# Attention and two expert layers on one core: another order at the start, tanh for sigmoid, column tiles, other buffers at two stage borders, a last product in halves

## The chip, the core and the metric

The kernel runs on one NeuronCore of one Trainium2 chip. A core has TensorE (matmuls; its weight loads are a row of their own in a profile, PEld), VectorE (DVE), ScalarE (ACT), GpSimd (POOL) and SyncE (SP), whose instruction queue issues most of the DMA transfers here. The metric is the time of one execution on the device in microseconds (us); the median of several runs counts.

## What is computed

All inputs and the output are float32 in the reference except that the weights arrive as float64 words. The kernel computes a linear attention and two expert layers behind it, for 8 x 576 = 4608 tokens:

```python
q_s = softmax(q, axis=-1)              # q, k, v: (8, 8, 576, 64): batch, head, token, 64
k_s = softmax(k, axis=2)               # over the tokens
kv  = einsum('bhsd,bhse->bhde', k_s, v)
x   = einsum('bhsd,bhde->bhse', q_s, kv)   # then (4608, 512)
h   = x @ w1_in                        # (4608, 2048)
g   = h * (1 / (1 + exp(-1.702 * h)))
x1  = g @ w1_out                       # (4608, 512)
h2  = x1 @ w2_in                       # (4608, 2048)
g2  = where(h2 >= 1, h2, where(h2 <= -1, 0, (h2 + 1)**2 / 4))
out = g2 @ w2_out                      # (4608, 512)
```

## The kernel before

All large products run on float32 split in a high and a low half (`split`, L103: ScalarE copies the high half, L104, VectorE subtracts to get the low half, L105), as three matmuls: high by high, high by low, low by high. A weight arrives as 64-bit words; `conv` (L85) makes float32 of it with one ScalarE copy (L92) and three VectorE operations (L94, L95, L99).

**First stage** (`x @ w1_in`, plain). Tokens come in 9 blocks j of 512, the 2048 columns of h in 16 groups m of 128; step s is (j, m), with twelve matmuls (`gemm1`, L767 to L769). After every second step `act` (L771) applies the sigmoid on ScalarE (L775), multiplies on VectorE (L776) and stores g. The attention of the next block is prepared beside the steps of the present one, by `chain` (L785), which puts each operation on a step: `load_k`, `k_max`, `k_col` (a transpose, then a maximum, L664), `k_sub` (L672), `k_exp` (L681); `load_v`; `k_v` (L683: per head pair, five matmuls of 128 rows of keys by 129 columns, two heads at once and a column of ones for the sum; the last of the five has 64 rows); `load_q`, `q1` (maximum and subtraction, L707 and L708), `q1e` (exponential, L711), `q2` (sum L716, reciprocal, multiply), `q3` (transposes and a copy), `q4` (matmuls px and a split). The exponentials are put on two steps per block, so that those between two sigmoids run together. For block 0 all of this stands ahead of the first step (L837 to L872). The weights of w1_in are loaded and converted in 16 groups (`load_w`, `conv_w`), the first ahead of the steps, the others in the steps of block 0. In later blocks the weights of the other three products are converted and combined by `weight_sets`.

**The other three products** (out1, in2, out2) use seven block products instead of eight (Winograd's form), named PROD = (1, 7, 6, 2, 5, 4, 3), on tokens in five pieces j (512, 512, 512, 384, 384 tokens per half). A pool of 27 numbered tiles (`slot`) holds all operands; which tile holds what is written out by hand (G_AT, R_AT, O_AT, C_AT, E_AT, L245 to L251). `out_pass(ph, ...)` (L297) is out1 (ph 0) and out2 (ph 1); a step is one product p and one inner quarter i, twelve matmuls at L338. `ready(s)` splits the operands of a step into two tiles, three steps ahead. For ph 1, steps 0 to 3 go to tiles 8 to 15, all later ones round R_AT[1]. `store` sends results out; in out2 it first transposes them (`turn`, L354), copies them into tile 23 (L365) and stores from there. `pass_in` (L434) is in2 with its matmuls at L456; it ends each result with `finish` (ScalarE L470, L471, VectorE L472), in the tiles 22 to 26 (E_AT) round, from which g1 is stored. Beside it the weights of out2 are loaded raw (`load_set`), converted and combined; these jobs stand at steps 14 + 14 i and on. The raw loads use one tile of the pool.

The order of instructions on each engine follows program order as far as a scheduler of the framework leaves it; `behind` ties one instruction behind another.

## Time and profile before

| | |
|---|---|
| median of 3 runs | 1609.55 us (1609.12 to 1614.41) |
| the profiled execution | 1607.64 us, its span 1605.8 us |
| TensorE busy | 1565.2 us (97%) |
| VectorE busy | 1150.5 us (72%) |
| ScalarE busy | 947.4 us (59%) |
| mean granted TensorE clock | 0.996 |
| HBM traffic | 205 GB/s over the span |

The span is the time from the first to the last instruction; some 2 us lie around it. Matmuls overlap, so TensorE's busy share says only where it had work in hand, and the distance from one matmul's start to the next says what one costs. A product step of 12 matmuls of 512 columns takes 2.72 us, of 384 columns 2.08 us.

### The profile page before, as it was taken

How to read it: one execution, taken by the hardware profiler on the slowest of the kernel's cores; microseconds unless marked ns; L12 is line 12 of the kernel's file. 1: busy time of each engine (PE TensorE's matmuls, PEld its weight loads, DVE VectorE, ACT ScalarE, POOL GpSimd, SP SyncE). 2: the span in 40 equal slices, each digit the busy share in tenths (PEclk: the TensorE clock that was granted, in tenths of full speed). 3: DMA queues.
4: the chain of work that ended last, by engine and by line, in shares of the span. 5: the costliest groups of instructions: out<-in, count | busy, mean ns of one | idle time of the engine just before them, and what ended most of it. 6: DMA issues, size and time to landing. Idle time of an engine off the chain costs nothing.

```text
span 1605.8 us, 20662 instructions
## 1 busy us (share of the span) xinstructions
PE 1565.2 (97%) x7588; PEld 1343.1 (84%) x7588; DVE 1150.5 (72%) x1519; ACT 947.4 (59%) x1135; POOL 8.1 (1%) x45
## 2 busy tenths in 40 slices
PE   5899999999999999999999999999999999999998
PEld 3678888888888888888999888878998788888998
DVE  7999788788833678686777686868454876766673
ACT  4877777776832444443545687868775444444453
POOL 0000000000000000000000000000000000000000
PEclk9999999999999999999999999999999999999999
DMA  8788788888767761715368766566547853424421
GB/s 209 217 249 273 257 269 267 275 264 266 254 240 280 270 210 65 225 45 177 101 206 327 274 217 248 203 220 236 193 165 296 328 185 105 157 84 138 131 68 40
DMA packets 218869, 330.61 MB, mean 206 GB/s; under 512 B 90128, under 2 KB 162832, under 8 KB 216080
## 3 DMA queue, kind: packets, MB, share of 16 engines
q1 hardware_dynamic: 218768, 329.30, 60.9%
q8 instruction: 59, 0.97, 0.2%
q14 instruction: 42, 0.34, 0.1%
HBM read 190.84 MB, written 138.41 MB: 205 GB/s over the span
## 4 chain that ended last, share of the span: by engine, by line
PE 89%; DMA 3%; DVE 2%; ACT 1%; issue 1%; SPq 0%; DVEq 0%; ACTq 0%
PE z L338 24%; PE zx L338 18%; PE z L456 10%; PE hps L767 8%; PE hps L769 8%; PE hps L768 8%; PE zx L456 7%; PE pk L689 2%; PE px L738 2%; DMA s<-in_moe_w_out_dram 1%; PE pt L361 1%; DMA g<-s 1%; PE pt L728 1%; DMA wp_out<-s 1%; DVE s L118 0%
## 5 line engine op out<-in xcount | busy, mean ns | idle before, releaser
L104 ACT ACTIVATE s<-s 128x1024 fp32r<-128x1024 f32 (+2 forms) x363 | 326.0, 901 | 370.9 <-PE z L338 177.7
L105 DVE TENSOR_TENSOR s<-s,s 128x1024 fp32r<-128x1024 f32 (+2 forms) x363 | 369.5, 1023 | 175.3 <-PE z L338 71.5
L338 PE MATMUL z<-s,w 128*128 128x512 f32 (+1 forms) x1920 | 404.0, 369 | 5.4 <-DVE s L105 3.3
L338 PEld LDWEIGHTS z<-s,w 128*128 128x128 f32 x1920 | 350.1, 188 | 51.2 <-DVE s L105 3.6
L338 PE MATMUL zx<-s,w 128*128 128x512 f32 (+1 forms) x1440 | 303.2, 368 | 0.0
L338 PEld LDWEIGHTS zx<-s,w 128*128 128x128 f32 x1440 | 261.7, 188 | 33.3
L767 PE MATMUL hps<-xh,w 128*128 128x512 f32 x576 | 237.6, 413 | 5.2 <-ACT w L104 4.6
L769 PE MATMUL hps<-xh,w 128*128 128x512 f32 x576 | 226.5, 393 | 1.1 <-DVE w L105 1.1
L768 PE MATMUL hps<-xl,w 128*128 128x512 f32 x576 | 225.9, 392 | 0.0
L118 DVE TENSOR_TENSOR s<-s,s 128x1024 f32<-128x1024 f32 (+2 forms) x196 | 205.8, 1058 | 21.5 <-DMA s<-g 17.1
L456 PE MATMUL z<-s,w 128*128 128x512 f32 (+1 forms) x960 | 206.9, 367 | 0.0
L456 PEld LDWEIGHTS z<-s,w 128*128 128x128 f32 x960 | 175.1, 188 | 22.6
L456 PE MATMUL zx<-s,w 128*128 128x512 f32 (+1 forms) x720 | 158.9, 369 | 2.8 <-DVE s L118 1.7
L456 PEld LDWEIGHTS zx<-s,w 128*128 128x128 f32 x720 | 130.5, 188 | 22.6 <-DVE s L118 3.9
L767 PEld LDWEIGHTS hps<-xh,w 128*128 128x128 f32 x576 | 108.8, 189 | 31.5 <-ACT w L104 5.6
L776 DVE TENSOR_TENSOR sg<-hps,sg 128x1024 f32<-128x1024 f32 x72 | 87.6, 1217 | 66.3 <-ACT sg L775 66.0
L769 PEld LDWEIGHTS hps<-xh,w 128*128 128x128 f32 x576 | 108.3, 188 | 25.9 <-DVE w L105 2.2
L768 PEld LDWEIGHTS hps<-xl,w 128*128 128x128 f32 x576 | 108.6, 189 | 21.2 <-issue 1.1
L775 ACT ACTIVATE sg<-hps 128x1024 f32<-128x1024 f32 x72 | 73.9, 1026 | 82.4 <-PE hps L769 82.0
L471 ACT ACTIVATE s<-s 128x1024 f32<-128x1024 f32 (+1 forms) x80 | 77.6, 971 | 1.5
L470 ACT ACTIVATE s<-s,half 128x1024 f32<-128x1024 f32 (+1 forms) x40 | 42.4, 1061 | 26.0 <-DVE s L118 25.8
L472 DVE SCALAR_TENSOR_TENSOR s<-s,s 128x1024 f32<-128x1024 f32 (+1 forms) x40 | 44.7, 1116 | 12.4 <-ACT s L471 12.0
(76 smaller groups left out, 1242.4 us busy)
## 6 DMA issues: line engine op xcount, KB each, us to landing
s<-g SPq DMA_DIRECT2D x96, 512.0 KB, 4.4
g<-sg SPq DMA_DIRECT2D x72, 512.0 KB, 3.2
w<-wp_out SPq DMA_DIRECT2D x14, 2048.0 KB, 12.8
g<-s SPq DMA_DIRECT2D x48, 512.0 KB, 2.8
s<-g SPq DMA_DIRECT2D x48, 384.0 KB, 3.8
wp_out<-w SPq DMA_DIRECT2D x28, 512.0 KB, 4.2
wp_in<-w SPq DMA_DIRECT2D x28, 512.0 KB, 3.9
w<-wp_in SPq DMA_DIRECT2D x7, 2048.0 KB, 8.3
```

Source lines behind the costliest of these rows:

```text
L104: nc.scalar.activation(out=hi, in_=src, func=ACTF.Copy)
L105: return nc.vector.tensor_tensor(out=lo, in0=src, in1=hi.bitcast(FP32), op=ALU.subtract)
L118: return nc.vector.tensor_tensor(out=o, in0=x, in1=y, op=op)
L338: nc.tensor.matmul(out=z[:, m, :n], lhsT=a, rhs=b[:, c, :], start=(p in OPENS and i == 0 and c == 0 and x == 0), stop=(i == 3 and c == 1 a ...
L456: nc.tensor.matmul(out=z[:, m, :n], lhsT=a, rhs=b[:, c, :], start=(p in OPENS and c == 0 and x == 0), stop=(c == 1 and x == 2), skip_group ...
L471: nc.scalar.activation(out=t, in_=t, func=ACTF.Square)
L472: nc.vector.scalar_tensor_tensor(out=t, in0=h, scalar=1.0, in1=t, op0=ALU.max, op1=ALU.min)
L767: nc.tensor.matmul(out=hps, lhsT=wh, rhs=xh[:, kk, :], start=(kk == 0), stop=False)
L768: nc.tensor.matmul(out=hps, lhsT=wh, rhs=xl[:, kk, :], start=False, stop=False)
L769: nc.tensor.matmul(out=hps, lhsT=wl, rhs=xh[:, kk, :], start=False, stop=(kk == KD - 1))
L775: nc.scalar.activation(out=sg, in_=hps, func=ACTF.Sigmoid, scale=1.702)
L776: nc.vector.tensor_tensor(out=sg, in0=hps, in1=sg, op=ALU.mult)
```

## The change

- *Start*: the loads of q and v for tiles 0 and 1 are issued from ScalarE's queue, all k loads come ahead of the first w1_in load on SP, the first weight conversion is tied behind the last subtraction of k of block 0, and the q tiles 1 and 2 take their exponentials per head on ScalarE with a bias and a sum (`q1s`).
- *Exponentials*: in `chain` each exponential stands one step behind its subtraction, on its own.
- *tanh for sigmoid*: the first layer stores h (tanh(0.851 h) + 1), twice the wanted value; out1's copies and additions multiply by 0.5.
- *Column tiles*: in `k_v` each head has its own matmul of 64 weight columns by 65 columns, the second head on the array's upper columns; v gets a column of ones per head.
- *in2*: jobs of the raw loads start at step 12 + 14 i, and each load stands two steps ahead of its conversion instead of one; the sums come a step earlier.
- *Entry of out2*: steps 0 to 5 have tiles of their own (4 and 5: 20, 21 and 24, 23) and the round behind them has another order.
- *End of out2*: the last product is computed for its first 128 rows (m = 0) over all four quarters, then for the others; each half is copied, transposed and stored by itself, the last one with ScalarE and VectorE side by side.

```diff
     def conv(raw, f, r):
-        nc.vector.tensor_scalar(out=r, in0=lw, ...)
+        first = nc.vector.tensor_scalar(out=r, in0=lw, ...)
...
+        return first
...
-    R_AT = ((16, 17, 18, 19, 24, 25, 26), (24, 25, 26, 8, 9, 10, 11))
+    R_AT = ((16, 17, 18, 19, 24, 25, 26), (8, 9, 10, 11, 25, 26, 24))
...
+        first_at = ((8, 9), (10, 11), (12, 13), (14, 15), (20, 21), (24, 23))
...
-            if ph and s < 4:
-                at = (8 + 2 * s, 9 + 2 * s)
+            if ph and s < len(first_at):
+                at = first_at[s]
+            elif ph and s >= len(steps) - 4:
+                at = (i, 16 + i)
             else:
-                k = 2 * (s - 4 * ph)
+                k = 2 * (s - len(first_at) * ph)
...
-        def gemm(s):
+        def gemm(s, ms=range(2)):
...
-            for m in range(2):
+            for m in ms:
...
         def turn():
-            for j, a, b, t in late:
+            for j, a, b, t, ms in late:
...
                 for r in range(4):
-                    for m in range(2):
+                    for m in ms:
...
-                nc.scalar.activation(out=u[:n4], in_=pt[:n4], func=ACTF.Copy)
+                d = slice(ms[0] * P, (ms[-1] + 1) * P)
+                if ms == (1,):
+                    nc.scalar.activation(out=u[:n4, :2, d], in_=pt[:n4, :2, d], func=ACTF.Copy)
+                    nc.vector.tensor_copy(out=u[:n4, 2:, d], in_=pt[:n4, 2:, d])
+                else:
+                    nc.scalar.activation(out=u[:n4, :, d], in_=pt[:n4, :, d], func=ACTF.Copy)
...
+        def close(m):
+            n = HALVES[-1]
+            z = zs["x"][:, m, :n]
+            t = tmp["c12"] = tmp["c12"] if m else slot(20)[:, :, :n]
+            c = n // 2 if m else n
+            nc.scalar.activation(out=t[:, m, :c], in_=z[:, :c], func=ACTF.Copy)
+            if m:
+                nc.vector.tensor_copy(out=t[:, m, c:], in_=z[:, c:])
+            late.append((NJ - 1, 0, 1, t, (m,)))
...
-                nc.scalar.activation(out=t, in_=z, func=ACTF.Copy)
+                nc.scalar.activation(out=t, in_=z, func=ACTF.Copy, scale=1.0 if ph else 0.5)
...
+            def more(t):
+                if ph:
+                    tt(t, t, z, ALU.add)
+                else:
+                    nc.vector.scalar_tensor_tensor(
+                        out=t, in0=z, scalar=0.5, in1=t, op0=ALU.mult, op1=ALU.add
+                    )
...
+                for m in range(2):
+                    for i in range(4):
+                        gemm(whole + i, (m,))
+                        if m == 0 and i == 0:
+                            ready(whole + 3)
+                        if i == 2:
+                            turn()
+                    close(m)
                 turn()
...
-            s0 = 14 + i * 14
+            s0 = 12 + i * 14
             for h in range(2):
-                jobs.setdefault(s0 + 2 * h, []).append((load_set, ("out2", i, h)))
-                jobs.setdefault(s0 + 2 * h + 1, []).append((convert_set, (h,)))
+                jobs.setdefault(s0 + 3 * h, []).append((load_set, ("out2", i, h)))
+                jobs.setdefault(s0 + 3 * h + 2, []).append((convert_set, (h,)))
             for part in range(4):
-                jobs.setdefault(s0 + 5 + part, []).append((sum_set, ("out2", i, part)))
+                jobs.setdefault(s0 + 6 + part, []).append((sum_set, ("out2", i, part)))
...
-        v_t = [vpool.tile([P, KR + 1, P + 1], FP32, name=f"v{i}") for i in range(HP)]
+        v_t = [vpool.tile([P, KR + 1, 2, D + 1], FP32, name=f"v{i}") for i in range(HP)]
...
-            conv(raw1(m), f, r)
+            behind(conv(raw1(m), f, r), st["sub"] if m == 0 else None)
...
-            follow(nc.scalar.activation(out=kt, in_=kt, func=ACTF.Exp), st.get(("sub", b)))
+            nc.scalar.activation(out=kt, in_=kt, func=ACTF.Exp)
...
-            pk = ps_a.tile([P, P + 1], FP32, tag="a", name="pk")
+            pk = ps_a.tile([P, D + 1], FP32, tag="a", name="pk")
             for r in range(KR + 1):
                 n = P if r < KR else KT
-                nc.tensor.matmul(
-                    out=pk,
-                    lhsT=kt[:n, r].rearrange("p h d -> p (h d)"),
-                    rhs=vt[:n, r, :],
-                    start=(r == 0),
-                    stop=(r == KR),
-                )
+                for h in range(2):
+                    nc.tensor.matmul(
+                        out=pk[h * D:(h + 1) * D],
+                        lhsT=kt[:n, r, h, :],
+                        rhs=vt[:n, r, h, :],
+                        start=(r == 0),
+                        stop=(r == KR),
+                        tile_position=(0, h * D),
+                        skip_group_check=True,
+                    )
...
+        def q1s(t):
+            qt = q_t[t]
+            mx = sm.tile([P, H], FP32, tag="qm", name="qm")
+            nc.vector.tensor_reduce(out=mx, in_=qt, axis=AX.X, op=ALU.max)
+            nc.vector.tensor_scalar(out=mx, in0=mx, scalar1=-1.0, scalar2=None, op0=ALU.mult)
+            z = st["qz", t] = sm.tile([P, H, 1], FP32, tag="qz", name="qz")
+            for h in range(H):
+                nc.scalar.activation(
+                    out=qt[:, h, :], in_=qt[:, h, :], func=ACTF.Exp, bias=mx[:, h:h + 1], accum_out=z[:, h]
+                )
...
-            nc.scalar.activation(out=sg, in_=hps, func=ACTF.Sigmoid, scale=1.702)
-            nc.vector.tensor_tensor(out=sg, in0=hps, in1=sg, op=ALU.mult)
+            nc.scalar.activation(out=sg, in_=hps, func=ACTF.Tanh, scale=0.851)
+            nc.vector.scalar_tensor_tensor(
+                out=sg, in0=sg, scalar=1.0, in1=hps, op0=ALU.add, op1=ALU.mult
+            )
...
-                    put(4.2 if i < 2 else 8.2, k_exp, b, i)
+                    put(2 * i + 3, k_exp, b, i)
...
-                put(4.3 if i < 2 else 8.3, q1e, t)
+                put(2 * i + 3.3, q1e, t)
...
-        load_k(0, 0)
-        load_k(0, 1)
+        for i in range(HP):
+            load_k(0, i)
+            if i < 2:
+                load_q(i, nc.scalar)
+                load_v(0, i, nc.scalar)
         load_w(0)
-        load_k(0, 2)
-        load_k(0, 3)
...
-        for i in range(HP):
+        for i in range(2, HP):
             load_q(i)
             load_v(0, i)
...
-            q1(i)
-            q1e(i)
+            if i in (1, 2):
+                q1s(i)
+            else:
+                q1(i)
+                q1e(i)
```

## Rows read from the trace of the kernel before

**Rows 1.** Stages: us; PE, PEld, DVE, ACT, POOL busy; clock; DMA share; GB/s.

```profile
0.00:38.18 38.18, 18.20 (x73) 12.80 (x73) 26.58 (x69) 16.70 (x31) 3.25 (x21) 0.96 0.82 206
38.18:103.31 65.13, 58.64 (x274) 45.35 (x273) 63.26 (x126) 50.80 (x72) 0.80 (x4) 1.00 0.78 233
103.31:533.90 430.59, 430.59 (x2046) 351.08 (x2045) 316.00 (x556) 280.27 (x359) 4.01 (x20) 1.00 0.79 265
533.90:878.70 344.80, 344.80 (x1680) 305.51 (x1680) 259.69 (x240) 161.49 (x170) 0.00 (x0) 1.00 0.51 174
878.70:1229.90 351.20, 348.42 (x1686) 305.68 (x1686) 235.34 (x302) 261.25 (x322) 0.00 (x0) 1.00 0.62 221
1229.90:1245.90 16.00, 10.67 (x46) 8.25 (x45) 7.14 (x8) 5.34 (x7) 0.00 (x0) 0.89 1.03 422
...
1598.70:1605.80 7.10, 1.08 (x8) 0.83 (x8) 0.00 (x0) 1.83 (x2) 0.00 (x0) 0.90 0.36 106
```

**Rows 2.** VectorE's waits, 0 to 38.15 us: waiter, releaser, us in total, times, longest.

```profile
DVE m L654 <- DMA kr<-in_k_dram: 4.1, 2, 3.7
DVE w L94 <- DMA w<-in_moe_w_in_dram: 2.8, 1, 2.8
DVE rs L697 <- PE pk L689: 2.6, 2, 1.4
DVE kt L672 <- PE pk L689: 1.1, 1, 1.1
```

**Rows 3.** Groups by line, whole span, then start: busy us, mean ns | idle.

```profile
L775 ACT ACT_TABLE_LOAD x39 | 50.0, 1283 | 0.7
...
L708 DVE TENSOR_TENSOR qt<-qt,qm 128x512 f32<-128x512 f32 x4 | 2.7, 670 | 0.0
```

**Rows 4.** Timeline of TensorE around a pk product: start, duration (us), engine, line, tiles.

```profile
191.72 1.47 PE L689 MATMUL pk<-v,kt 128*128 128x129 f32 x10
...
192.28 0.49 PE L689 MATMUL pk<-v,kt 128*128 128x129 f32 x3
...
192.70 0.49 PE L689 MATMUL pk<-v,kt 64*128 64x129 f32 x2
...
193.45 0.40 PE L769 MATMUL hps<-xh,w 128*128 128x512 f32 x1
```

**Rows 5.** Timeline of a 64-column matmul pair; groups of weight loads by shape.

```profile
91.11 0.33 PE L738 MATMUL px<-qT,kv 128*128 128x64 f32 x2
...
L361 PEld LDWEIGHTS pt<-ident,s 128*128 128x128 f32 x96 | 11.2, 140 | 1.5
...
L361 PEld LDWEIGHTS pt<-ident,s 128*96 128x96 f32 x64 | 7.2, 126 | 1.6 <-ACT s L385 1.2
```

**Rows 6.** VectorE's waits in the in2 stage; the chain there (start, us, what).

```profile
DVE s L94 <- DMA s<-in_moe_w_out_dram: 22.2, 11, 4.6
...
908.84 2.72 PE zx L456 x12
...
920.75 4.75 DMA s<-in_moe_w_out_dram
```

**Rows 7.** Entry of out2: chain, timeline (idle before, releaser), stretches with clock.

```profile
1230.68 13.87 DMA g<-s
...
1242.13 0.50 PE L338 MATMUL z<-s,w 128*128 128x512 f32 x1 [2.06 <-ACT s L104]
...
1245.93 12.53 PE L338 MATMUL z<-s,w 128*128 128x512 f32 x47 [3.30 <-DVE s L105]
...
1245.90:1249.30 3.40, 3.37 (x8) 2.70 (x9) 3.40 (x4) 1.75 (x2) 0.00 (x0) 0.50 0.95 407
1249.30:1252.70 3.40, 3.40 (x16) 2.81 (x16) 3.40 (x4) 2.13 (x2) 0.00 (x0) 0.99 0.98 405
```

**Rows 8.** Timeline of the end.

```profile
1598.73 0.81 ACT L385 ACTIVATE s<-zx 128x768 f32<-128x768 f32 x1 [1.04 <-PE zx L338]
...
1600.83 1.02 ACT L365 ACTIVATE s<-pt 96x1024 f32<-96x1024 f32 x1 [1.29 <-DMA out_dram<-s]
```

More of the change, by code (lines that the diff above doesn't have):

```diff
@@ L92, in conv @@
         nc.scalar.activation(out=f, in_=hwf, func=ACTF.Copy, scale=2.0 ** -112)
-        nc.vector.tensor_scalar(out=r, in0=lw, scalar1=2.0 ** -29, scalar2=7.0, op0=ALU.mult, op1=ALU.min)
+        first = nc.vector.tensor_scalar(
+            out=r, in0=lw, scalar1=2.0 ** -29, scalar2=7.0, op0=ALU.mult, op1=ALU.min
+        )
         nc.vector.scalar_tensor_tensor(
@@ L329, in gemm @@
             z = zs[Z_OF[p]]
-            hi, lo = ops.pop(s)
+            hi, lo = ops[s]
             w = sl[p]
-            for m in range(2):
+            for m in ms:
                 for c in range(2):
@@ L351, in store @@
             else:
-                late.append((j, a, b, t))
+                late.append((j, a, b, t, (0, 1)))
         def turn():
-            for j, a, b, t in late:
+            for j, a, b, t, ms in late:
                 n, t0 = HALVES[j], STARTS[j]
@@ L397, in post @@
             elif p == 5:
-                tt(tmp["s7"], tmp["s7"], z, ALU.add)
+                more(tmp["s7"])
                 store(j, 1, 1, tmp["s7"])
             elif p == 4:
-                tt(tmp["u2"], tmp["u2"], z, ALU.add)
+                more(tmp["u2"])
                 store(j, 1, 0, tmp["u2"])
@@ L410, in run @@
                 ready(s)
-            for s, (j, p, i) in enumerate(steps):
+            whole = len(steps) - 4 * ph
+            for s, (j, p, i) in enumerate(steps[:whole]):
                 gemm(s)
@@ L599, with load_tokens @@
         k_t, q_t, st = {}, {}, {}
-        def load_tokens(dst, src, together):
+        def load_tokens(dst, src, together, eng):
             if together:
-                nc.sync.dma_start(out=dst[:, :, :KR], in_=src[:, :KR * P].rearrange("h (p r) d -> p h r d", r=KR))
+                eng.dma_start(out=dst[:, :, :KR], in_=src[:, :KR * P].rearrange("h (p r) d -> p h r d", r=KR))
             else:
                 for i in range(2):
-                    nc.sync.dma_start(out=dst[:, i, :KR], in_=src[i, :KR * P].rearrange("(p r) d -> p r d", r=KR))
-            nc.sync.dma_start(out=dst[:KT, :, KR], in_=src[:, KR * P:].rearrange("h p d -> p h d"))
+                    eng.dma_start(out=dst[:, i, :KR], in_=src[i, :KR * P].rearrange("(p r) d -> p r d", r=KR))
+            eng.dma_start(out=dst[:KT, :, KR], in_=src[:, KR * P:].rearrange("h p d -> p h d"))
         def load_k(b, hp):
@@ L630, in segs, with load_q @@
                 done += n
-        def load_q(t):
+        def load_q(t, eng=nc.sync):
             qt = qpool.tile([P, H, D], FP32, tag="q", name="qt")
             for off, n, b, s in segs(t * P, P, S):
-                nc.sync.dma_start(
+                eng.dma_start(
                     out=qt[off:off + n], in_=q[b, :, s:s + n, :].rearrange("h p d -> p h d")
@@ L638, in load_q @@
             q_t[t] = qt
-        def follow(ins, other):
-            if other is not None:
-                tc.add_manual_dep(
-                    getattr(ins, "ins", ins),
-                    getattr(other, "ins", other).name,
-                    mybir.DependencyInfo(mybir.DependencyClass.NoSync, mybir.DependencyReason.DATA),
-                    reason="exponentials together",
-                )
         def k_max(b, hp):
@@ L701, in k_v @@
                 o = slice(j * D, (j + 1) * D)
-                nc.scalar.activation(out=kv[o, hp, o], in_=pk[o, o], func=ACTF.Copy, scale=rs[o])
+                nc.scalar.activation(out=kv[o, hp, o], in_=pk[o, :D], func=ACTF.Copy, scale=rs[o])
         def q1(t):
@@ L714, in q2 @@
             qt = q_t[t]
-            z = sm.tile([P, H, 1], FP32, tag="qz", name="qz")
-            nc.vector.tensor_reduce(out=z, in_=qt, axis=AX.X, op=ALU.add)
+            z = st.pop(("qz", t), None)
+            if z is None:
+                z = sm.tile([P, H, 1], FP32, tag="qz", name="qz")
+                nc.vector.tensor_reduce(out=z, in_=qt, axis=AX.X, op=ALU.add)
             nc.vector.tensor_scalar(out=z, in0=z, scalar1=EPS, scalar2=None, op0=ALU.add)
```

18 lines of the change are left out of this document (9 added, 9 removed).

## The prediction

> **What bounds the kernel now.** The stage table comes first [rows 1]: it splits the span by stage and shows which engine has no slack in each. TensorE is busy for all of 103.3 to 533.9 us and all of the out1 product (533.9 to 878.7), at a full clock, so there only its own instructions count and faster neighbours buy nothing. It is not full in four places, and the change works on all four. Until 38.18 us the first token block is prepared and no product runs; VectorE works 26.58 of these 38.18 us. From 38.18 to 103.31 us, the sixteen column groups of the first block, TensorE is busy 58.64 of 65.13 us while VectorE is busy 63.26: here VectorE is the bound. The in2 stage takes 351.2 us where out1, the same 1680 matmuls, takes 344.8. After it TensorE idles over 5 us at the entry of the last product, and 7.1 us follow its last matmul. The waits name the causes, and come next.
>
> **How times are counted.** The sum is made against the profiled execution: 1607.6 us, of which 1605.8 are the span. The median of the runs is 1609.55, 1.9 above it; what the sum takes off is taken off the median.
>
> **Start and first block.** In program order VectorE would do the four k tiles first; in the trace it stood 2.8 us at L94, the first weight group's conversion, until its load landed, with k work queued behind it; 2.6 us at L697 and 1.1 us at L672 it waited for the pk products [rows 2]. The new tie of that conversion behind the last k subtraction takes the 2.8 us away. The pk product needs v, and the v and q loads of tiles 0 and 1 now start at once on ScalarE's queue instead of after nine other issues on SP's; I count all of the 1.1 us and half of the 2.6 us. What is moved: eight DMA issues onto ScalarE ahead of its first exponential (it is idle there, so I cost them at nothing; were it busy they would cost its work their issue time), and on SP the first w1_in load now stands behind all k loads, which hurts nobody since its conversion is moved too. Tiles 1 and 2 take their exponentials on ScalarE with bias and sum: VectorE loses two subtractions (670 ns) and two sums of the same size [rows 3] and gains two tiny operations, 2.4 us net; ScalarE gets 16 short instructions for 2 long ones, beside idle time. ScalarE also drops table loads of 1.28 us each [rows 3] in the first block, where TensorE's idle time is mostly for weights that ScalarE copies. But what it copies comes from VectorE, which has under 2 us of slack in this stage [rows 1]; table loads alone give little, and I count nothing. A DMA rule of the Trainium skill (DMA: Bandwidth & Descriptors, "Rules for kernel authors") speaks against the second load queue: issuing from several engines saves issue time only, since the same 16 DMA engines carry all. The trace bears it out in that these engines are already 0.82 busy in this stretch [rows 1]; by it the queue would give only order, which is all that I count. Sum: 2.8 + 1.1 + 1.3 + 2.4 = 7.6 us. Because VectorE also bounds the block that follows, this moves the whole rest of the program. Bounds: 1 (VectorE meets other waits instead) to 10.3 us (38.18 - 26.58 = 11.6 of idle time, less the 3.7 until k first lands [rows 2], and the 2.4).
>
> **Column tiles.** One pk product is ten matmul records (float32 goes in two passes). From the first at 191.72 to the second GEMM matmul behind it, less that one's own 0.23, it costs 193.45 - 0.23 - 191.72 = 1.50 us [rows 4]. Records lie 0.11 apart (three take 0.49 with the last one's 0.27 in it), ten are 1.10. The other 0.40 is the change of shape at the two 64-row records and back: 0.20 for each change. Now each record becomes two of 65 columns on 64 weight columns. A 64-column moving matmul takes 0.06 (two in 0.33, less 0.27) [rows 5], and weight loads get shorter with their columns (140 ns at 128, 126 at 96). So twenty records take 1.12 one after the other; three changes of shape instead of two (full, 64 columns, 64 by 64, full) take 0.60; together 1.72. If the two halves of the array run fully side by side, ten slots of 0.056 and 0.60 give 1.16. No row shows two parts of the array in use at once, so nothing is nearer to one end; I take the middle, 1.44. There are 28 such groups beside the full TensorE (32 less the four of the start): (1.44 - 1.50) x 28 = -1.7 us, between -9.5 and +6.2.
>
> **Sigmoid by tanh, exponentials early.** The 72 ScalarE calls and 72 VectorE products keep their size; the halving goes into copies at out1 that exist already. If exp and tanh do share a table, ScalarE loses the 39 loads at L775, 50.0 us [rows 3], and about as many ahead of the exponentials. From 103 us on it all lies beside a TensorE that never waits: 0. If they do not share one, loads come back more often, still beside TensorE (ScalarE is busy 280 of 431 us there).
>
> **In2 stage.** Of 351.2 - 344.8 = 6.4 us, 1.4 are six matmuls of the last stage that already run in it (1686 for 1680); about 5 are lost. VectorE stood 22.2 us, 11 times, for raw weight loads (L94) [rows 6]; and the chain of waits goes through such loads (one issued at 920.75 takes 4.75 us). A load is issued one step (12 matmuls, 2.72 us [rows 6]) ahead of its conversion. The change makes it two steps, 5.4 us, longer than a load takes: 4.0 of 5 come back. Queued behind the second load on SP, which now waits for the first conversion as before, are the g1 stores; they have five tiles and nobody waits for them. Bounds 2 and 5.
>
> **Entry of the last stage.** Step 4 puts its operands into tiles 24 and 25, whose g1 stores are still under way: a store issued at 1230.68 lands 13.87 us later, with the DMA engines full (share 1.03) [rows 1, 7]. TensorE waits 2.06 and 3.30 us. After it idled it runs at a granted clock of 0.50, the lower of its two levels (1.2 GHz): 8 matmuls in 3.4 us against 16 in the next 3.4, 1.7 lost [rows 7]. With the restarts that is 7.6 us. Tiles 20 and 21 are free with in2's last product, and 25 and 26 are not asked for until step 8, 4 x 2.72 us later, when that store is long down. I count 7.2; bounds 3 (ScalarE still puts the start product's copy first and TensorE waits for one split) and 7.7.
>
> **Tail.** The copy of the last product shrinks from 0.81 us to halves on two engines (about 0.4), eight transposes to four, the 1.02 us copy out to about 0.4 [rows 8], 1.5 less. The halves' times are my estimates from the whole ones. But the staging tile 23 is one: the second half's copy waits for the first half's store, which is issued about when TensorE ends; before, too, the copy out waited 1.29 us for the store ahead of it [rows 8]. I take 0.9, between 0.2 and 1.6.
>
> **Sum.** -7.6 - 1.7 - 4.0 - 7.2 - 0.9 = -21.4 us: 1586.2 for the profiled execution, **1588.2** on the median; pk's ends alone make it 1580 to 1596.
>
> **Rivals.** *The halves run fully side by side.* The Trainium skill (TensorEngine Tiling (Array Packing), "Key Properties") says that tiles load weights and multiply in parallel, and that a change of mode drains the engine; the trace agrees with the second (0.20 us a change), no row shows the first. As a mechanism of this kernel: pk at 1.16, -9.5 in place of -1.7, 1580.4. Against it: records follow one another in order [rows 4], and each half has two passes in a row. *Weight loads keep their time with half the columns.* Then twenty records at 0.11 and 0.60 are 2.80 a group, +36.4 us; with the other gains 1609.55 + 36.4 - 19.7 = 1626.3, slower. It decides from 2.20 us a group (no gain left) and 2.38 (slower beyond measurement). Against it are the 126 and 140 ns; for it, that these are latencies, not spacings. *VectorE takes back the start.* The block's bound stays where it is, since its order is a scheduler's and new waits appear: 1 instead of 7.6, 1594.8. *The entry keeps its gap*, at step 4 or 5, from weights or operands that land as late as the store did (DMA full): 0 instead of 7.2, 1595.4. For it, the DMA share [rows 1]; against it, TensorE's only waits there were for the two splits. That tanh needs a table of its own is the change not doing what it says; it would move only the first block, by a few us, and is inside the range.
>
> **Chances.** Forecast 0.52, full overlap 0.18, VectorE 0.13, entry 0.09, slow weight loads 0.08. A measurement of this kernel tells about 0.3%, 4.8 us, from no change. Faster: all but the last, less 0.06 for two losses together, 0.86; same 0.06; slower 0.08. Range: low, full overlap with 2.7 us more from the start, 1577.7, so 1577; high, serial tiles with the start lost, 1609.55 - 1 + 6.2 - 4 - 7.2 - 0.9 = 1602.7, so 1604.
>
> **What would show it.** First GEMM matmul near 31 us instead of 38.18, the second block's near 95 instead of 103.31; no VectorE wait at L94 before 38 us; one table load left; pk groups of 1.2 to 1.7 us; in2 within 2 us of 344.8; no TensorE gap and no 0.50 clock between the last two stages; a tail of about 6 us. A pk group above 2.2 us would make the prediction wrong by itself, a start that stays near 38 would halve it.

## The result, and the profile after

The changed kernel takes 1590.05 us (median of 4 runs, 1588.83 to 1592.94) against 1609.34 for the kernel before beside it (4 runs): a ratio of 0.988, 95% interval 0.986 to 0.990. The forecast was 1588.2, faster. The profiled executions are 1590.52 and 1607.64 us, 17.1 apart; of these 17.1 us the ledger below is made. Each stage is measured from the start of its first matmul in one trace to that in the other.

| us | before | after | difference | predicted |
|---|---|---|---|---|
| first px matmul at | 35.04 | 35.03 | 0.0 | |
| first GEMM matmul at | 38.18 | 40.00 | +1.8 | near 31 |
| first block, from there | 65.14 | 61.20 | -3.9 | start and block together -7.6 |
| rest of the first pass | 430.41 | 422.35 | -8.1 | -1.7 |
| out1 | 344.99 | 344.99 | 0.0 | 0 |
| in2 | 350.49 | 350.55 | +0.1 | -4.0 |
| out2 up to its last 48 matmuls | 360.11 | 353.27 | -6.8 | -7.2 |
| from there to the end | 16.53 | 16.38 | -0.15 | -0.9 |

So the total came within 2 us on the median (on the profiled executions the forecast was 1586.2, a miss of 4.3) by misses that largely cancel: the start gave less than a third of what I counted, in2 nothing, and the column tiles nearly five times their term.

The stages of the changed kernel, as in [rows 1] (interval; busy time of TensorE, its weight loads, VectorE, ScalarE, GpSimd; granted clock; DMA share; GB/s):

```profile
0.00:40.00 40.00, 18.89 (x112) 11.44 (x113) 25.28 (x68) 21.14 (x62) 3.56 (x21) 1.00 0.86 230
40.00:101.20 61.20, 57.36 (x314) 43.09 (x313) 59.91 (x121) 35.81 (x59) 0.80 (x4) 1.00 0.78 238
101.20:523.60 422.40, 422.40 (x2286) 337.12 (x2285) 315.84 (x560) 195.37 (x293) 4.45 (x20) 1.00 0.80 268
868.50:1219.80 351.30, 348.67 (x1687) 305.86 (x1686) 235.29 (x302) 261.68 (x323) 0.00 (x0) 1.00 0.62 222
1219.80:1235.80 16.00, 15.62 (x69) 12.60 (x68) 13.17 (x13) 8.38 (x10) 0.00 (x0) 1.00 1.02 419
```

TensorE is still full from the second block on, in 422 us instead of 430; in2 is as it was; at the entry of out2 TensorE works 15.62 of 16 us, where it worked 10.67, with the DMA engines as full as before.

The waits at the start, 0 to 40 us, as in [rows 2]:

```profile
DVE rs L730 <- PE pk L720: 3.7, 3, 1.2
DVE kt L702 <- PE pk L720: 0.7, 1, 0.7
ACT w L92 <- DMA w<-in_moe_w_in_dram: 3.2, 1, 3.2
DVE qm L747 <- DMA qt<-in_q_dram: 2.8, 2, 1.8
```

VectorE's 2.8 us at L94 are gone, and 2.8 us for q tiles stand in their place; its waits for pk products grew from 3.7 us (2.6 and 1.1) to 4.4 (3.7 and 0.7). ScalarE, whose half of the conversion was not tied, still waits 3.2 us for that weight load; before it waited 6.5 us, but with no exponential ready behind it.

TensorE at the end of the start (start, duration, line, tiles), in the changed kernel:

```profile
33.04 1.11 PE L775 MATMUL pt<-ident,qt 128*128 128x128 f32 x4
35.03 5.53 PE L785 MATMUL px<-qT,kv 128*128 128x512 f32 x8 [0.88 <-ACT qT L780]
40.00 0.79 PE L814 MATMUL hps<-xh,w 128*128 128x512 f32 x1
```

and in the kernel before:

```profile
35.04 3.70 PE L738 MATMUL px<-qT,kv 128*128 128x512 f32 x8 [0.70 <-ACT qT L733]
38.18 0.80 PE L767 MATMUL hps<-xh,w 128*128 128x512 f32 x1
```

px starts at the same time in both and takes 1.8 us longer for the same matmuls. That is TensorE's lower clock level, and it is what the first GEMM matmul lost. The clock column above reads 1.00 there, but the profile of the run without `q1s` (below) has a stretch with 0.50 over the same work, where px to the first GEMM matmul takes 5.1 us, as the 4.97 here, and not 3.1:

```profile
26.10:39.70 13.60, 8.80 (x53) 5.49 (x52) 11.75 (x30) 7.73 (x16) 0.00 (x0) 0.50 0.76 205
```

### The profile page after: what moved, and what is told of

The parts are those of the page before. It is cut to its first block, busy times and chain, and to the rows that moved or that the text cites. A ratio compares the mean times of both kernels' runs of the same rounds, so it can differ in the third digit from the quotient of the medians.

```text
span 1588.7 us, 21246 instructions
## 1 busy us (share of the span) xinstructions
PE 1555.3 (98%) x7908; PEld 1324.5 (83%) x7908; DVE 1146.4 (72%) x1519; ACT 850.9 (54%) x1090; POOL 8.8 (1%) x45
## 3 DMA queue, kind: packets, MB, share of 16 engines
q10 hardware_dynamic: 4480, 1.11, 0.3%
## 5 line engine op out<-in xcount | busy, mean ns | idle before, releaser
L824 DVE SCALAR_TENSOR_TENSOR sg<-sg,hps 128x1024 f32<-128x1024 f32 x72 | 87.7, 1218 | 61.5 <-ACT sg L823 59.7
```

The lines of the kernel that those rows point to most:

```text
L824: nc.vector.scalar_tensor_tensor(out=sg, in0=sg, scalar=1.0, in1=hps, op0=ALU.add, op1=ALU.mult)
```

## The experiments

Every run is the changed kernel but for what is named; the edits are shortened. The runs from *fill* to *the same, one queue*, and the last, have matmuls of no use in the start. All but the changed kernel and the last were executed once. The stage times, from the traces as above (px and GEMM: when the first one starts):

| run | px | GEMM | first block | rest of pass | in2 | out2 | end | execution |
|---|---|---|---|---|---|---|---|---|
| changed kernel | 35.03 | 40.00 | 61.20 | 422.35 | 350.55 | 353.27 | 16.38 | 1590.52 |
| pk whole | 33.82 | 36.96 | 63.36 | 430.89 | 347.35 | 353.29 | 16.38 | 1595.04 |
| heads apart | 40.47 | 45.60 | 63.84 | 441.66 | 348.72 | 353.29 | 16.38 | 1616.26 |
| no q1s | 35.81 | 40.89 | 61.65 | 422.28 | 349.89 | 353.30 | 16.37 | 1591.14 |
| fill | 32.94 | 36.07 | 61.06 | 422.35 | 350.92 | 353.27 | 16.38 | 1586.83 |
| fill, both tied | 34.03 | 37.17 | 61.44 | 422.36 | 350.69 | 353.27 | 16.38 | 1588.11 |
| fill, one queue | 32.44 | 35.58 | 64.53 | 425.70 | 349.44 | 353.27 | 16.56 | 1591.84 |
| fill, sums late | 34.04 | 37.18 | 61.02 | 422.34 | 352.36 | 353.27 | 16.38 | 1589.34 |
| sums late, less fill | 31.80 | 36.64 | 63.11 | 422.35 | 349.37 | 353.27 | 16.39 | 1587.90 |
| the same, one queue | 32.35 | 38.19 | 66.09 | 427.61 | 348.06 | 353.27 | 16.66 | 1596.64 |
| later parts undone | 33.83 | 39.46 | 63.93 | 426.04 | 349.45 | 360.01 | 16.53 | 1602.22 |
| second raw tile | 35.70 | 40.85 | 62.80 | 422.37 | 352.44 | 355.45 | 16.38 | 1597.05 |
| sums late, fill in three places | 31.91 | 35.05 | 61.51 | 422.37 | 351.25 | 353.29 | 16.38 | 1586.62 |

How far a single run can be read: the changed kernel and the run with a second raw tile have the same first pass, and differ by 0.7 us at px and 1.6 us in the first block. The 0.7 lie ahead of the first pk product (18.95 and 19.62 us; from there to px both take 16.08), and in its first block the second one has a stretch at the lower clock that the changed kernel has not:

```profile
70.50:73.90 3.40, 3.40 (x9) 2.64 (x8) 2.54 (x7) 1.72 (x4) 0.00 (x0) 0.50 0.79 245
```

Such a stretch stands in seven of the runs, among them all with a first block over 61.6 us but *pk whole* and *heads apart*. In2, untouched in ten runs besides the changed kernel, takes 347.4 to 352.4 us; the rest of the pass repeats to 0.1 where the loads, the pk products and tanh stay as they are, and out2 where its tiles do.

### Column tiles undone

```diff
-    for h in range(2): nc.tensor.matmul(out=pk[h * D:(h + 1) * D], lhsT=kt[:n, r, h, :], rhs=vt[:n, r, h, :], tile_position=(0, h * D), ...)
+    nc.tensor.matmul(out=pk, lhsT=kt[:n, r], rhs=vt[:n, r, :], ...)
```

> The changed kernel with the column tiles alone undone: each pk product is ten matmuls of 129 columns again, and v and its ones column lie as before. In the changed kernel a pk group costs 0.99 us and the second block to the end of the first pass takes 422.3 us, in the kernel before 1.52 us and 430.4 us. Theory: the two halves of the array multiply side by side, and that is the whole gain of the steady first pass: the groups go back to 1.52 us, that stretch to 430 to 432 us, the first block (with its four groups) up by 2, and the execution to about 1600 us. Rival: the gain there is from the missing table loads and the exponentials in their new places; then the stretch stays at 422 to 424 us and the execution at 1591 to 1593.

The rest of the pass goes back to 430.89 us: the whole gain there is the column tiles'. The first block goes up by 2.2, as expected, but two runs of the same first block differ by 1.6. Against the kernel before (430.41), which differs in this stretch by sigmoid and the places of the exponentials, it is within 0.5 us: those two are worth nothing there. What was not expected: the first GEMM matmul comes 3.0 us earlier without the column tiles. TensorE's start there:

```profile
22.47 2.65 PE L719 MATMUL pk<-v,kt 128*128 128x129 f32 x10
26.73 0.63 PE L772 MATMUL pt<-ident,qt 128*128 128x128 f32 x4 [1.60 <-DVE qt L763]
33.82 3.70 PE L782 MATMUL px<-qT,kv 128*128 128x512 f32 x8 [0.70 <-ACT qT L777]
```

The pk products take 2.65 us each at the lower clock, not 1.55, and the transposes behind the second of them take 0.63 us, not 1.09: the clock had risen. That the longer products kept TensorE busy enough for it is the near explanation, but it is not shown: in the next run they are longer still, and the clock stays low.

### The two heads one after the other

```diff
-    for r in range(KR + 1):
-        for h in range(2):
+    for h in range(2):
+        for r in range(KR + 1):
```

> The changed kernel with the order of the 20 half matmuls of a pk product changed: all of the first head's, then all of the second head's. The same instructions on the same shapes, but neighbours use the same half of the array. Theory (the halves run side by side because neighbours lie in different halves): a pair costs twice a single one, 20 records at about 0.058 are 1.16 and the group goes from 0.99 to about 1.5 us, the first pass up by about 28 x 0.5 = 14 us, the execution to 1603 to 1606 us. Rival (a half matmul is simply cheap, 0.03 us each): group and time stay, 0.99 us and 1590 us.

One pk product in the changed kernel, and here:

```profile
186.95 0.95 PE L720 MATMUL pk<-v,kt 128*64 128x65 f32 x20
187.83 0.50 PE L814 MATMUL hps<-xh,w 128*128 128x512 f32 x1
188.17 0.39 PE L815 MATMUL hps<-xl,w 128*128 128x512 f32 x1
```

```profile
415.80 1.80 PE L720 MATMUL pk<-v,kt 128*64 128x65 f32 x20
417.53 0.50 PE L814 MATMUL hps<-xh,w 128*128 128x512 f32 x1
417.86 0.40 PE L815 MATMUL hps<-xl,w 128*128 128x512 f32 x1
```

Read as in the prediction, from the first record to the second GEMM matmul less 0.23: 188.17 - 186.95 - 0.23 = 0.99 us against 417.86 - 415.80 - 0.23 = 1.83. The same twenty records cost nearly twice as much when neighbours lie in the same half of the array (in the program's order there are two more changes of shape in the 1.83); the pass is 19.3 us longer, where I had expected 14. So the halves run side by side, and only because their records alternate. In the start a pk product takes 2.99 us here, and the eight px records still run at the lower clock:

```profile
22.60 2.99 PE L720 MATMUL pk<-v,kt 128*64 128x65 f32 x20
40.47 5.69 PE L785 MATMUL px<-qT,kv 128*128 128x512 f32 x8 [0.87 <-ACT qT L780]
```

### The exponentials with bias and sum undone

```diff
-            if i in (1, 2): q1s(i)
-            else: q1(i); q1e(i)
+            q1(i); q1e(i)
```

> The changed kernel with the exponentials with bias and sum of q tiles 1 and 2 undone: a subtraction on VectorE, one exponential, and a sum on VectorE, as for tiles 0 and 3. Theory (in the start no engine is full, and the chain goes pk product, its row sum on VectorE, the next q tile, its transposes, the next pk product): the 2.4 us that VectorE takes back fall partly into its waits for the pk products; the first px matmul moves from 35.0 to 35 to 36.5 us. Rival (VectorE's work sets the start): it moves by 2.4 us, to 37.4. Second rival (ScalarE, which has 16 short exponentials of 0.33 in place of two of 0.63, sets it): it moves down by 1 to 3 us.

px moves by 0.8 us, hardly more than two runs of the same start differ; from the first pk product it takes 16.58 us instead of 16.08. The 2.4 us of VectorE's work that I counted in full were at most a third on the path.

### Filling TensorE's gaps

```diff
             k_v(0, i)
+            if i in (1, 2): 10 or 14 matmuls of the identity by itself into an unused bank, tied behind pk
```

> The changed kernel with 10 and 14 matmuls of no use on the identity put behind the second and the third pk product, where TensorE idles 2.3 and 2.7 us. Theory: the start lost 1.8 us because TensorE's clock was still at its lower level at px (0.853 us between two px matmuls against 0.429 in the kernel before, which had it full from 30.8 us); with TensorE kept busy the clock is full before px, px to the first GEMM matmul is 3.1 us instead of 4.97, and that matmul comes at 38.1 to 38.7 us instead of 40.0; the execution at about 1589. Rival: px is slow for another reason, its operands or the DMAs at 1.1 of full; then it stays at 4.9 us and the added work delays pk by up to 1 us.

```profile
30.18 0.60 PE L775 MATMUL pt<-ident,qt 128*128 128x128 f32 x4
32.94 3.70 PE L785 MATMUL px<-qT,kv 128*128 128x512 f32 x8 [0.69 <-ACT qT L780]
36.07 0.80 PE L814 MATMUL hps<-xh,w 128*128 128x512 f32 x1
```

With work that computes nothing the GEMM starts 3.9 us earlier: 1.8 in px, as expected, and 2.1 ahead of it, which I had not expected; the transposes and pk products of the chain run at the full clock too (0.60 us for four transposes, not 1.11). So the lower clock cost the start 3.9 us. What the preparation gained by itself does not follow from this run, since the kernel before ran part of its start at the lower clock too (0.96 over it, [rows 1]).

### ScalarE's half tied as well

```diff
-        nc.scalar.activation(out=f, in_=hwf, func=ACTF.Copy, ...)
+        top = nc.scalar.activation(...); behind(top, last k exponential)
```

> The changed kernel with the matmuls of no use of the run before (first px matmul at 32.94 us, first GEMM matmul at 36.07, span 1585.0), and ScalarE's half of the first weight group's conversion also tied behind the last exponential of a k tile. In the changed kernel ScalarE stood 3.2 us at that half, for its load, with the first k exponential queued behind it. Theory A (that wait is on the path of the start: the wait that the change took from VectorE came back on ScalarE): the first k exponential comes at 11.3 us instead of 14.7 and the first px matmul 1 to 3 us earlier than 32.94. Theory B (the first pk product waits in TensorE's order behind the last pb transpose at 18.5 us, which VectorE's wait for q tile 2 sets, and not for the exponentials): px stays within 0.5 us of 32.94.

The first k exponential comes at 11.81 us instead of the fill run's 14.28, and px not earlier but 1.1 us later (34.03), outside theory B's 0.5. Its reason holds: ScalarE's wait was not on the path, since the first pk product (19.32 us) follows the last pb transpose on TensorE (18.91), which came later with a later q tile 2.

### One load queue

```diff
-                load_q(i, nc.scalar)
-                load_v(0, i, nc.scalar)
+                load_q(i)
+                load_v(0, i)
```

> The changed kernel with the matmuls of no use (px at 32.94 us, first GEMM matmul at 36.07), and the v and q loads of tiles 0 and 1 issued on SP again, in the changed kernel's order, so that the second load queue alone is undone. Theory (the queue gives order only): 8 issues of 0.4 to 0.8 us go back to SP ahead of its other loads, w_in and q tiles 2 and 3 land about 4 us later, ScalarE is free for its first exponential, and px moves to 33 to 35 us. Rival (the queue is what makes k, q and v land early): px at 36 us or later. Second rival (ScalarE's issues cost its work): px below 32.5 us.

px is 0.5 us earlier than with both queues: below the 33 us of the theory and just at the second rival, but no more than two runs of the same start differ. The second queue brought nothing. ScalarE's table load runs at 0.74 us instead of 9.49, the first pk product starts at 16.73 us instead of 18.52, and this lead is lost to q tile 2, whose first operation on VectorE moves from 14.73 to 21.45 us. The first block is 3.5 us longer and the rest of the pass 3.4, of which TensorE's new gaps at 376 and 420 us are 0.7 and 1.1: the instructions of the later blocks stand in another order than in the fill run.

### The row sums out of the chain

```diff
             k_v(0, i); q2(i); q3(i)
+            if i: k_n(0, i - 1)       # row sum and normalisation, taken out of k_v
```

> The changed kernel with the matmuls of no use (px at 32.94 us, first GEMM matmul at 36.07), and the row sum and normalisation of a pk product moved behind the next q tile's last step and transposes, so that VectorE no longer stands at L730 for a pk product (1.2 us, three times) ahead of the q work which the next transposes and, behind them on TensorE, the next pk product wait for. Theory (the start is a chain through the in-order queues: pk, its row sum, the next q tile, its transposes, the next pk): px 2 to 4 us earlier, 29 to 31 us, the first GEMM matmul at 32 to 34. Rival (VectorE's work sets the start, wherever it waits): px within 0.7 us of 32.94.

No gain by itself: px at 34.04, later than either side had it; 0.8 of the 1.1 us lie ahead of the first pk product (19.30 us instead of 18.52). But VectorE had finished q tile 1 at 23.4 us instead of 24.7, while TensorE worked at the fill until 26.65. So the order was tried again with less fill:

> The changed kernel with the row sum and normalisation of a pk product behind the next q tile's last step (as in the run before with it), but with only 8 matmuls of no use, behind the third pk product. In that run VectorE had the q tiles done at 23.4 and 27.1 us while TensorE was still at its useless matmuls until 26.6 and 31.3 us, so these hid what the order brought. Theory (the chain through the in-order queues sets the start): the second transposes come at 23.4 to 24 us instead of 25.5, the third at 27 to 28 instead of 30.2, and px at 29.5 to 32 us; if the clock is still at its lower level there, px to the first GEMM matmul takes 4.9 us instead of 3.1. Rival (other work of VectorE and ScalarE is in the way just as well): px at 33 us or later, as with the row sums ahead.

px comes at 31.80 us, 1.1 before the run with the row sums in place and 3.2 before the changed kernel, as the theory of the chain pk, row sum, q tile, transposes, pk has it. It is not shown apart: this run has less fill too, and none has 8 matmuls with the row sums in place. And the clock fell before px; the stretches there (columns as above):

```profile
28.00:32.20 4.20, 1.09 (x8) 0.72 (x6) 3.48 (x13) 3.62 (x9) 0.00 (x0) 1.00 0.74 198
32.20:35.60 3.40, 3.40 (x5) 1.35 (x4) 2.37 (x4) 1.59 (x3) 0.00 (x0) 0.50 0.99 260
35.60:39.00 3.40, 3.40 (x13) 2.21 (x12) 2.83 (x5) 2.42 (x5) 0.00 (x0) 1.00 1.05 300
```

TensorE had worked 1.09 of the 4.2 us ahead of it. With one queue and a later tie of the first conversion:

> As the run above it (row sums behind the next q tile, 8 matmuls of no use), with all first loads on SP again, and with the first conversion of weights tied behind the third q tile's last step instead of the last k subtraction. With the loads on SP the first exponential came at 6.7 us instead of 10.3 and the first pk product at 16.7 instead of 18.5 us. Theory (ScalarE's queue of loads delayed its table load and first exponential, and the conversions lie in the chain): the first pk product at 16.5 to 17.2 us, px at 28 to 30.5 us, the first GEMM matmul at 32 to 34.5. Rival (the q tiles 2 and 3, which land later from SP, take the chain's place): px at 31.5 us or later.

px at 32.35: the rival. The first pk product came at 16.77 us, but q tile 2's exponentials only at 22.87, behind its later load.

### The later parts undone

```diff
-            nc.scalar.activation(out=sg, in_=hps, func=ACTF.Tanh, scale=0.851)
+            nc.scalar.activation(out=sg, in_=hps, func=ACTF.Sigmoid, scale=1.702)
-                    put(2 * i + 3, k_exp, b, i)
+                    put(4.2 if i < 2 else 8.2, k_exp, b, i)
...
-            s0 = 12 + i * 14
+            s0 = 14 + i * 14
...
-    R_AT = ((16, 17, 18, 19, 24, 25, 26), (8, 9, 10, 11, 25, 26, 24))
+    R_AT = ((16, 17, 18, 19, 24, 25, 26), (24, 25, 26, 8, 9, 10, 11))
-        first_at = ((8, 9), (10, 11), (12, 13), (14, 15), (20, 21), (24, 23))
+        first_at = ((8, 9), (10, 11), (12, 13), (14, 15))
...
-            whole = len(steps) - 4 * ph
+            whole = len(steps)
```

> The changed kernel with four of its parts put back as they were, each of which lies in a stage of its own: sigmoid in place of tanh and the exponentials of the first pass at their grouped places; the times of the raw loads in the in2 stage; the operand tiles at the entry of the last stage; the last product in one piece. The start with its orders, queues and column tiles stays. Theory, by stage (changed kernel in brackets): tanh lies beside a TensorE that never waits, so the first pass after its first block stays at 422 to 423 us (422.35); the loads of the in2 stage are held by their one raw tile, so that stage stays at 349.5 +- 2 (350.5); the entry tiles are worth the whole gain of the last stage, which goes to 360 us up to its last 48 matmuls (353.27); the halves of the last product give back what they save, so the end from there takes 16.5 us (16.38). Rivals: the first pass goes to 425 us or more (ScalarE with its table loads comes into TensorE's way); the in2 stage goes to 353 or more (the moved loads brought their 4 us, and something else took them); the end goes to 17.3 (the halves are worth 0.9).

out2 goes to 360.01 us, so the entry tiles are worth 6.7; the end to 16.53, so the halves are worth 0.15; in2 to 349.45, no worse than with the moved loads, though a run of it can be read to 5 us only. The rest of the pass goes to 426.04, which is the rival's side, by one stop:

```profile
253.85 0.63 ACT L107 ACTIVATE w<-w 128x512 fp32r<-128x512 f32 x1 [4.58 <-DMA wp_out<-w]
259.01 0.70 PE L776 MATMUL px<-qT,kv 128*128 128x256 f32 x2 [3.35 <-ACT qT L771]
```

TensorE waited there for a copy by ScalarE. This run has 80 table loads where the changed kernel has one, but they did not make that copy late at first hand: from 245.93 to 259 us no table load ran, and ScalarE stood 4.58 us for a store of weights (`wp_out`) to leave the tile that it had to write, with the copy some operations behind. Unlike the kernel before, this run has no tie that keeps exponentials together. So the 3.7 us are not what tanh brought.

### A second raw tile in in2

```diff
-        128, [wr[0]], [wr[1]...
+        128, [wr[0], slot(26)...], [wr[1]...         # E_AT without 26
```

> The changed kernel with a second raw tile for the weight loads of the in2 stage (tile 26, which the stage's results give up: they have four tiles instead of five), so that every second load waits for no conversion and no store out of the shared tile. In the changed kernel the loads were issued at the same times after the start of the stage as in the kernel before (4.0 and 20.4 us for the first two), though the program has them a step earlier. Theory (what held a load was the one raw tile, not its place in the program): the second loads of the pairs come several us earlier, VectorE's wait at L94 falls from 22.4 us to 10 or less, and the stage from 350.5 us to 346 to 348.5. Rival (SP's order behind the g1 stores held them): the wait at L94 stays over 18 us and the stage within 1.5 us of 349.5, the mean of the four runs with this stage untouched (347.4 to 350.9). Second rival (four result tiles are too few): the stage takes over 352 us.

In the changed kernel the loads leave SP at the times after the stage's start at which they left before, as a pair from SP's queue shows; here 904.79 and 910.56, with the stage's start at 868.54, are 36.25 and 42.02 us:

```profile
904.79 0.49 SPq L143 DMA_DIRECT2D s<-in_moe_w_out_dram  x1
907.32 2.46 SPq L515 DMA_DIRECT2D g<-s  x2
910.56 0.33 SPq L143 DMA_DIRECT2D s<-in_moe_w_out_dram  x1
```

and in the kernel before, with its start at 878.71, 36.27 and 42.04:

```profile
914.98 0.49 SPq L140 DMA_DIRECT2D s<-in_moe_w_out_dram  x1
917.50 2.46 SPq L475 DMA_DIRECT2D g<-s  x2
920.75 0.33 SPq L140 DMA_DIRECT2D s<-in_moe_w_out_dram  x1
```

With the second tile the second load leaves at 886.09, 15.1 us after the stage's start (871.00) where it left 20.4 us after it in both other kernels:

```profile
886.09 0.43 SPq L143 DMA_DIRECT2D s<-in_moe_w_out_dram  x1
```

VectorE's wait goes as expected, and the stage does not shrink. The waits of in2, in the changed kernel:

```profile
DVE s L94 <- DMA s<-in_moe_w_out_dram: 22.4, 10, 4.9
```

and with the second tile:

```profile
ACT s L510 <- DMA g<-s: 8.7, 6, 2.5
DVE s L94 <- DMA s<-in_moe_w_out_dram: 6.7, 5, 2.0
```

15.7 us less of VectorE's waiting, but 8.7 us more of ScalarE's for a result tile, and the stage takes 352.4 us, of which 1.92 are one gap of TensorE at its end; out2 is 2.2 us longer too. Over 352 is the second rival's sign, and untouched runs of the stage reach 352.4 as well, so this run cannot say what the loads alone would bring. The raw tile did hold the loads; that VectorE's wait for them is what TensorE lost is not shown: that step of the prediction rested on the length of a wait, not on who waited for it. Which waits make TensorE's idle time in the stage (351.20 - 348.42 = 2.8 us before [rows 1], 351.30 - 348.67 = 2.6 after) stays open.

### Both causes of the start together

```diff
+            if i > 1: fill(10 if i == 2 else 8)     # behind the third and fourth pk product
             q2(i); q3(i)
+            if i == 3: fill(5)
+            if i: k_n(0, i - 1)
```

> The changed kernel with the two things put together that moved the start: row sums and normalisation of the pk products behind the next q tile's last step, and 10, 8 and 5 matmuls of no use on the identity in the three places where TensorE waits before px (behind the third and the fourth pk product and the last transposes). In the run with 8 of them px began at 31.80 us but at the lower clock (granted 0.5 from 32.2 to 35.6 us), and px to the first GEMM matmul took 4.8 us. Theory (the two causes add up): px at 31.5 to 32.3 us, the clock full from about 22 to 24 us on without a fall before px, the first GEMM matmul at 34.7 to 35.5 us, against 40.0 in the changed kernel, the first block at 61 to 63 us, the execution at 1585 to 1588 us, ratio to the kernel before 0.985 to 0.987. Rival (the useless matmuls stand in the way of the transposes): px at 33 us or later and a time over 1588.

```profile
31.91 3.70 PE L791 MATMUL px<-qT,kv 128*128 128x512 f32 x8
35.05 0.80 PE L827 MATMUL hps<-xh,w 128*128 128x512 f32 x1
```

All as the theory has it: 1586.62 us (5 runs, 1585.66 to 1589.08), ratio to the kernel before 0.985 (0.983 to 0.987). The first GEMM matmul is 4.95 us earlier than in the changed kernel, and the median 3.4 us below that kernel's, whose own runs were made beside other runs of the kernel before; the intervals of the two ratios overlap.

## Why the prediction held, and where it did not

**Start and first block** (-7.6, measured -2.1, inside the bounds of 1 to 10.3). The step that failed is "the new tie takes the 2.8 us away". The wait was taken away; its time was not, because VectorE's order then met 2.8 us for q tiles and 0.7 more for pk products. That was my rival "VectorE takes back the start", for about half of the sum. The second missing step is the clock: I weighed the shorter pk product only beside the full TensorE, and not in the start, where TensorE is half idle; its clock stayed at the lower level there, which cost 3.9 us. That the shorter product is the cause is not settled (whole products: clock up, px early; heads apart: longer products, clock low). As the changed kernel stands, the preparation's edits brought nothing: the 2.1 us are no more than the 2.2 that the column tiles took off the first block. With the clock kept, the second block starts at 97.1 us, 6.2 before 103.3, so about 4 of 7.6 come with a full clock; the run with whole pk products, whose clock rose as well, starts it at 100.3, which gives 3.0. The load queue (counted 2.4) is worth nothing measurable, q1s (2.4) at most 0.8. The signs fell with it: GEMM at 40.0 and not near 31, the second block at 101.2 and not near 95; no wait at L94 before 38 us and one table load, as said.

**Column tiles** (-1.7; measured -8.1 in the rest of the pass and 2.2 in the first block). The full overlap, a rival at 0.18, is what happens, and 0.99 us a group is below even its 1.16; the two measured parts, 10.3 us together, lie beyond the 9.5 of the term's own bound. Two terms were mis-sized: twenty records take ten slots of 0.058 us, where I took the middle between ten slots and twenty; and the changes of shape cost 0.99 - 0.58 = 0.41 us together, as the fewer ones of [rows 4] did (0.40), not 0.60. No row could tell the first, so the range had to hold it, and its low end (1577) did. The upper bound, 1.72 for halves one after the other, was near: the heads-apart run takes 1.83, with more changes of shape. The rest of the pass has 24 groups, and 24 x 0.53 = 12.7 us went from them, but 8.1 arrived: five groups are now cut in two by GEMM matmuls, at about 0.4 us each (2.13 us with three GEMM matmuls of 0.23 in it, against 0.99 to 1.05), and px products take 1.2 us more in all; some 1.4 us are not traced. The Trainium skill (TensorEngine Tiling (Array Packing), "Key Properties") has tiles working in parallel; by the two rows of pk above this trace agrees, for records that alternate between the halves.

**tanh and the early exponentials** (0): right, by the run with whole pk products (430.89 against 430.41). The cover I named, a ScalarE busy 280 of 431 us, is thinner than its share says: in the run with the later parts undone one copy of ScalarE's came late behind a store and stopped TensorE for 3.35 us.

**In2** (-4.0; measured +0.1, in a stage that spreads over 5 us from run to run; the sign, within 2 us of 344.8, was missed). The step "a load is issued one step ahead of its conversion, the change makes it two" failed: its place in the program never set the issue. The load waits in SP's queue for the one raw tile, and left at the same 36.3 and 42.0 us after the stage's start. I read the wait at L94 correctly and took its releaser's place in the program for its cause.

**Entry** (-7.2; measured -6.8): right, by its own steps. TensorE's start into out2:

```profile
1219.78 13.12 PE L344 MATMUL z<-s,w 128*128 128x512 f32 x57
1233.28 8.00 PE L344 MATMUL z<-s,w 128*128 128x512 f32 x34 [0.38 <-DVE s L108]
```

The waits of 2.06 and 3.30 us [rows 7] are one of 0.38, at step 5, and the granted clock stays at 1.00.

**Tail** (-0.9, bounds 0.2 to 1.6; measured -0.15). The sign was met, 6.0 us from the start of the last product matmul to the end instead of 7.5 (compare [rows 8]), but it was the wrong place to measure: the halves cost 1.3 us ahead of it.

```profile
1577.61 0.49 ACT L390 ACTIVATE s<-zx 128x384 f32<-128x384 f32 x1
1578.16 3.39 PE L344 MATMUL zx<-s,w 128*128 128x384 f32 x18 [0.58 <-ACT s L390]
1581.38 0.60 PE L367 MATMUL pt<-ident,s 128*96 128x128 f32 x4
1584.87 0.38 ACT L373 ACTIVATE s<-pt 96x256 f32<-96x256 f32 x1 [1.45 <-DMA out_dram<-s]
```

The second half's matmuls wait 0.58 us for the copy of the first, which lies in the same bank tile, and the first half's transposes now stand between the product's matmuls (0.4 us). The staging tile's wait, which I had counted, is there too (1.45 us).

**The sum** held because -6.4 us on the rest of the first pass stood against +5.5 on the start and first block, +4.1 on in2 and +1.1 on entry and tail. That these misses largely cancel is luck; of the terms, the entry, tanh and the zero of out1 came out by their own steps.

## What to carry to other kernels

A wait that is taken away is worth what then ends last: before counting it, follow the in-order queues to the next thing that the engine, and whoever waits for it, will meet. The clock of a partly idle TensorE can change with its work: here it stayed low when the products became shorter, and rose when the gaps were filled. So look at the durations of the same matmul before and after and not only at the work. Where a load waits for the buffer it overwrites, as in in2, moving it in the program does nothing until that buffer is free earlier.

## What the hardware showed that I had not expected

- Two matmuls of 64 weight columns in different halves of the array run side by side if their records alternate: 20 float32 records of 65 columns in 0.95 us, against 1.80 when the same records come one half after the other.
- What raises the clock is not settled by these runs. With the heads apart TensorE was busy for 6.96 of the 6.97 us from 18.63 to 25.6 us, and the eight px records at 40.5 us still took 5.69 us, against 3.70 at the full clock; with one queue the clock was up from 20.3 us on, after 3.57 us of similar work without a gap. The page's clock column reads 1.00 over the changed kernel's start, where px runs at the speed that is granted 0.50 elsewhere; the durations decide.
- An exponential with a sum out is two instructions on ScalarE, 337 and 187 ns for 64 columns (16 of each); at their pace of 0.33 us a head a q tile takes 2.7 us, where one exponential of 512 columns takes 0.62.
- Eight DMA issues on ScalarE, some with waits between them, stood ahead of its first table load until 9.02 us and of its first exponential until 10.31; without them these ran at 0.74 and 6.74.
